# Rows of a routed expert turned later on TensorE, first weights of the second expert loaded ahead, and the last expert ended tile by tile

## The chip, the core and the metric

The kernel runs on one core of a Trainium2 chip. The core has a matrix engine (TensorE, in the rows PE, its weight loads PEld), VectorE (DVE), ScalarE (ACT), GpSimd (POOL) and SyncE (SP), which run side by side and wait for each other by semaphores. Each engine takes its instructions strictly in the order in which they stand in its program. SP issues most transfers, POOL the indirect ones (a list of row numbers says which rows are read or written). The metric is the device time of one launch in microseconds, lower is better; the median of three runs is given.

## The reference

A windowed attention, then a gated feed-forward layer, then a layer of eight experts of which each token uses two. The change lies at the joint of the second and the third and at the end of the third:

```python
g = xn @ w_gate                                # feed-forward, d_ff 1536
x = (g * sigmoid(g) * (xn @ w_val)) @ w_out    # 1536 tokens x 512
logits = x @ w_gate2 + log1p(exp(x @ w_noise)) * noise
top2, top2_w = two best of 8 experts, softmax over the two
for e in range(8):
    h = maximum(x[mask_e] @ w1[e], 0)          # 512 -> 1024
    out[mask_e] += top2_w * (h @ w2[e])        # 1024 -> 512
```

Every product is taken as three fp32r products (high and low halves of both operands).

## The kernel before

The feed-forward layer visits groups of 256 or 512 tokens with a chunk of its 12 weight blocks at a time; the last visit (`VISITS[-1]`, tokens 1280 to 1535, blocks 8 to 11) makes for each block f a product with `w_gate` and one with `w_val` (`up`, 12 matmuls each, L646), the gate on ACT and DVE (`hidden`), and one visit later the product with `w_out` (`down`, L672). After a group's last block `route` picks the experts of its tokens and scatters token number and weight into `metad`, one slot for each token and expert.

The experts are run as `Unit`s. Unit 0 holds the first 256 slots of the expert that led after three of the five groups, so that it can start while the last tokens are still being routed; unit 1 holds that expert's other 256 slots and needs the last group (`late_slots`). Units 2 to 8 are the other experts in order of their number of tokens (`order`), with 480 down to 368 slots. A unit's steps, whose names the rows use:

- `fetch` (L853): SP reads its slots from `metad` into `me`; `slots` (L862): POOL makes row numbers `ic`;
- `gather` (L871): POOL issues one indirect transfer of 128 rows of `x2d` into `xg`, for each tile of slots;
- `turn` (L881): four PE transposes of `xg` into a PSUM bank `pg`, then ACT makes the high half `gh` (L883) and DVE the low half `gl` (L884);
- `run`: for f in 0 to 7 an `up` (12 matmuls into `pz`, L907, that read `gh` and `gl` of all the unit's slots), ReLU into `zh`, `zl`, and one step later a `down` into `ac` (L929, or L923 in units of the wide form); then the weighting `y` (L961, L964) and the indirect write of `y` into the output (L965).

`moe2_weights` has SP load the 256 KB slabs of `w1` (L837) and `w2` (L840) for one f; `late` reads all seven expert numbers on SP (L1059). The calls `side(f)` put the next unit's fetch, gathers, turns and weights between the steps of the running one. That is only the order of priority: the tile scheduler builds the program of each engine by a simulated timeline of its own, so an instruction stands where that timeline had its inputs ready. `follow(a, b)` ties instruction a behind b on the same engine.

Three buffers matter: four `xg` tiles shared by consecutive units, two PSUM banks for `pg` (tags t and o), and 19 weight slabs.

## Time and profile before

| | us |
|---|---|
| median of three runs (818.26 to 821.02) | 820.84 |
| the profiled execution | 815.08 |
| its span | 812.9 |
| PE busy | 778.2 (96%) |
| DVE, ACT, POOL busy | 459.6, 362.6, 312.9 |

The span is from the first to the last instruction of the profiled execution; 2.2 us of its time lie around it. PE is busy 96% of the span, with matmuls whose ends are modelled, so what can be read exactly is where it stood idle and who released it. The granted clock is a mean over a stretch: 1.00 is 2.4 GHz and 0.50 is 1.2 GHz.

### The profile page before, as it was taken

How to read it: one execution, taken by the hardware profiler on the slowest of the kernel's cores; microseconds unless marked ns; L12 is line 12 of the kernel's file. 1: busy time of each engine (PE TensorE's matmuls, PEld its weight loads, DVE VectorE, ACT ScalarE, POOL GpSimd, SP SyncE). 2: the span in 40 equal slices, each digit the busy share in tenths (PEclk: the TensorE clock that was granted, in tenths of full speed). 3: DMA queues.
4: the chain of work that ended last, by engine and by line, in shares of the span. 5: the costliest groups of instructions: out<-in, count | busy, mean ns of one | idle time of the engine just before them, and what ended most of it. 6: DMA issues, size and time to landing. Idle time of an engine off the chain costs nothing. (4 is left out here: it accounts for less than half of the span.)

```text
span 812.9 us, 13827 instructions
## 1 busy us (share of the span) xinstructions
PE 778.2 (96%) x5041; PEld 696.2 (86%) x5041; DVE 459.6 (57%) x1053; ACT 362.6 (45%) x807; POOL 312.9 (38%) x353
## 2 busy tenths in 40 slices
PE   8999999999899999999997996999999999999993
PEld 5789999999788888899996985888999999999982
DVE  4489866667487887334453575533545454545541
ACT  5677656656443443123332463433333434344430
POOL 7437742232285565002421335342424343524311
PEclk9999999999999999999999999999999999999997
DMA  8465421260242330010108005973363728272010
GB/s 187 106 165 146 118 65 28 45 190 15 79 130 93 118 100 0 1 52 27 27 9 242 25 18 159 330 240 120 104 207 114 246 89 269 87 234 75 36 37 34
DMA packets 116838, 88.76 MB, mean 109 GB/s; under 512 B 49449, under 2 KB 100649, under 8 KB 116768
## 3 DMA queue, kind: packets, MB, share of 16 engines
q1 hardware_dynamic: 107920, 65.43, 28.7%
q0 software_dynamic: 7120, 19.27, 7.1%
q10 hardware_dynamic: 1728, 3.15, 1.3%
q8 instruction: 41, 0.67, 0.4%
q14 instruction: 29, 0.24, 0.1%
HBM read 75.18 MB, written 13.34 MB: 109 GB/s over the span
## 5 line engine op out<-in xcount | busy, mean ns | idle before, releaser
L907 PE MATMUL pz<-gh,sa 128*128 128x256 f32 (+7 forms) x576 | 157.6, 340 | 0.8 <-ACT gh L883 0.8
L907 PEld LDWEIGHTS pz<-gh,sa 128*128 128x128 f32 x576 | 104.2, 190 | 6.2 <-ACT gh L883 1.0
L907 PE MATMUL pz<-gl,sa 128*128 128x256 f32 (+7 forms) x288 | 97.8, 339 | 0.9 <-DVE gl L884 0.9
L672 PE MATMUL acc<-wo,dh 128*128 128x512 f32 x288 | 88.3, 400 | 0.8 <-ACT dh L658 0.8
L923 PE MATMUL ac<-zh,sb 128*128 128x480 f32 (+4 forms) x320 | 86.3, 364 | 0.0
L911 ACT ACTIVATE zh<-pz 128x256 fp32r<-128x256 f32 (+7 forms) x72 | 35.1, 487 | 110.0 <-PE pz L907 110.0
L912 DVE SCALAR_TENSOR_TENSOR zl<-pz,zh 128x256 fp32r<-128x256 f32 (+7 forms) x72 | 39.8, 553 | 75.1 <-ACT zh L911 74.8
L646 PE MATMUL pz<-xTh,wg 128*128 128x256 f32 x352 | 73.7, 288 | 1.2 <-ACT xTh L550 1.0
L646 PE MATMUL pz<-xTh,wv 128*128 128x256 f32 x352 | 73.9, 288 | 0.1
L628 ACT ACTIVATE sa<-wab 128x512 fp32r<-128x512 f32 x72 | 45.2, 629 | 57.9 <-PE ac L923 40.5
L632 DVE TENSOR_TENSOR sa<-wab,sa 128x512 fp32r<-128x512 f32 x51 | 36.6, 720 | 45.5 <-ACT sa L628 45.3
L646 PEld LDWEIGHTS pz<-xTh,wg 128*128 128x128 f32 x352 | 58.4, 192 | 3.5 <-ACT xTh L550 1.2
L923 PEld LDWEIGHTS ac<-zh,sb 128*128 128x128 f32 x320 | 57.9, 188 | 3.2
L672 PEld LDWEIGHTS acc<-wo,dh 128*128 128x128 f32 x288 | 51.3, 189 | 9.7 <-ACT dh L658 1.4
L646 PEld LDWEIGHTS pz<-xTh,wv 128*128 128x128 f32 x352 | 58.4, 192 | 0.8 <-ACT wv L599 0.5
L659 POOL TENSOR_TENSOR dl<-u,dh 128x256 fp32r<-128x256 f32 (+1 forms) x38 | 37.8, 996 | 53.0 <-ACT dh L658 44.7
L907 PEld LDWEIGHTS pz<-gl,sa 128*128 128x128 f32 x288 | 54.8, 190 | 3.8 <-DVE gl L884 1.1
L871 POOL DMA_INDIRECT xg<-x2d,ic x30 | 30.5, 1018 | 67.7 <-PE pg L881 61.3
L812 POOL DMA_INDIRECT metad<-meta,si x24 | 24.3, 1012 | 83.4 <-DVE si L791 77.3
L672 PE MATMUL acc<-wo,dl 128*128 128x512 f32 x144 | 53.0, 400 | 0.2 <-POOL dl L659 0.2
L923 PE MATMUL ac<-zl,sb 128*128 128x480 f32 (+4 forms) x160 | 52.9, 357 | 0.0
L632 DVE TENSOR_TENSOR sb<-wab,sb 128x512 fp32r<-128x512 f32 x67 | 47.1, 703 | 8.9 <-ACT sb L628 8.0
(268 smaller groups left out, 1872.4 us busy)
## 6 DMA issues: line engine op xcount, KB each, us to landing
wab<-in_moe_w_dram SPq DMA_DIRECT2D x128, 256.0 KB, 4.9
rg<-in_moe_w_gate_dram SPq DMA_DIRECT2D x12, 512.0 KB, 3.7
rv<-in_moe_w_val_dram SPq DMA_DIRECT2D x12, 512.0 KB, 3.7
ro<-in_moe_w_out_dram SPq DMA_DIRECT2D x12, 512.0 KB, 3.5
vn<-in_v_dram SPq DMA_DIRECT2D x12, 256.0 KB, 4.4
out_dram<-zero SPq DMA_DIRECT2D x1, 3072.0 KB, 12.8
x2d<-x ACTq DMA_DIRECT2D x12, 256.0 KB, 3.6
kn<-in_k_dram SPq DMA_DIRECT2D x11, 256.0 KB, 3.9
```

What stands on the lines that cost most here:

```text
L628: cp = nc.scalar.activation(wp[:, 0], src, AF.Copy)
L632: (nc.gpsimd if pool else nc.vector).tensor_sub(wp[:, 1], src, wp[:, 0].bitcast(F32))
L646: nc.tensor.matmul(pz, a[:, cs], x[:, tt:tt + nt, c, :], start=(n == 0), stop=(n == 3 * DC - 1))
L659: (nc.gpsimd if ci < len(CHUNKS) - 1 else nc.vector).tensor_sub(dl, u, dh.bitcast(F32))
L672: nc.tensor.matmul(acc[t], a[:, tt], w, start=(f == CHUNKS[ci][0] and n == 0), stop=(end and n == 2))
L812: st = nc.gpsimd.indirect_dma_start(out=metad, out_offset=bass.IndirectOffsetOnAxis(ap=si[:, t, kk:kk + 1], axis=0), in_=meta[:, G0[g] + t ...
L871: self.last = nc.gpsimd.indirect_dma_start(out=xg[:m], out_offset=None, in_=x2d[:self.rows], in_offset=bass.IndirectOffsetOnAxis(ap=self.i ...
L907: nc.tensor.matmul(pz[:, :cap], a[:, cs], x[:, c, :cap], start=(k == 0), stop=(k == 3 * DC - 1))
L911: nc.scalar.activation(dh[:, :cap], pz[:, :cap], AF.Relu)
L912: nc.vector.scalar_tensor_tensor(dl[:, :cap], pz[:, :cap], 0.0, dh[:, :cap].bitcast(F32), op0=ALU.max, op1=ALU.subtract)
L923: nc.tensor.matmul(acc[c][:, :cap], w[:, c * P:(c + 1) * P], a[:, :cap], start=(f == 0 and k == 0), stop=(f == FB2 - 1 and k == 2))
```

## The change

- `turn` takes a matmul `behind` and ties its transposes to it. Unit 0's two turns go from the places kx 3 and 4 (blocks 8 and 9 of the last visit) to blocks 10 and 11, each behind that block's last `w_val` product. Unit 2's four turns, which were asked for from f = 4 on, go behind the last `up` product of unit 1 at f = 6 (two) and f = 7 (two). Turns of the other units are asked for as before.
- `late` reads only one expert number and at once loads four f of unit 2's weights (eight slabs), before unit 2's slots are fetched. The other six numbers are read when their unit is first asked for.
- In the last unit (8, three tiles of slots) the third tile's columns are cut in two halves with a PSUM bank each, and the `down` products of f = 6 and 7 are held and issued tile by tile: tiles 0 and 1 for f = 6, then for f = 7, then the third tile's first half for both f, then its second half. The weighting of the third tile becomes two DVE instructions.

```diff
@@ -643,8 +643,9 @@
         for c in range(DC):
             cs = slice(c * P, (c + 1) * P)
             for a, x in ((wh, xTh[g]), (wh, xTl[g]), (wl, xTh[g])):
-                nc.tensor.matmul(pz, a[:, cs], x[:, tt:tt + nt, c, :], start=(n == 0), stop=(n == 3 * DC - 1))
+                mm = nc.tensor.matmul(pz, a[:, cs], x[:, tt:tt + nt, c, :], start=(n == 0), stop=(n == 3 * DC - 1))
                 n += 1
+        return mm.ins
 
     def hidden(ci, f, t0, nt, pg, pv):
         GN = nt * P
@@ -872,13 +873,15 @@
                 out=xg[:m], out_offset=None, in_=x2d[:self.rows], in_offset=bass.IndirectOffsetOnAxis(ap=self.ic[:m, s:s + 1], axis=0))
             self.xg[s] = xg
 
-        def turn(self, s):
+        def turn(self, s, behind=None):
             m = self.tiles[s][1]
             xg = self.xg.pop(s)
             pt = ps.tile([P, 512], F32, name=f"pg{self.n}_{s}", tag="to"[s % 2])
             p3 = pt.rearrange("p (a b) -> p a b", a=DC)[:, :, :m]
             for c in range(DC):
-                nc.tensor.transpose(p3[:, c, :], xg[:m, c * P:(c + 1) * P], ident[:m, :m])
+                mm = nc.tensor.transpose(p3[:, c, :], xg[:m, c * P:(c + 1) * P], ident[:m, :m])
+                if behind is not None:
+                    follow(mm.ins, behind)
             ss = slice(s * P, s * P + m)
             nc.scalar.activation(self.gh[:, :, ss], p3, AF.Copy)
             nc.vector.tensor_sub(self.gl[:, :, ss], p3, self.gh[:, :, ss].bitcast(F32))
@@ -892,9 +895,14 @@
 
         def run(self, side):
             n, cap, gh, gl = self.n, self.cap, self.gh, self.gl
+            ending = n == E and len(self.tiles) < 4
+
+            def cuts(s):
+
+                return (slice(0, DM // 2), slice(DM // 2, DM)) if ending and s + 1 == len(self.tiles) else (slice(0, DM),)
             wide = cap % P > 0 and cap > 2 * P and n < 8
             acc = [ps.tile([P, 512], F32, name=f"ac{n}_{s}", tag=("d", "d", "t2", "s")[s], bufs=(2, 2, 1, 1)[s])
-                   for s in range(DC if wide else len(self.tiles))]
+                   for s in range(DC if wide else len(self.tiles) + ending)]
             self.ys = {}
 
             def up(f):
@@ -904,8 +912,9 @@
                 for c in range(DC):
                     cs = slice(c * P, (c + 1) * P)
                     for a, x in ((wh, gh), (wh, gl), (wl, gh)):
-                        nc.tensor.matmul(pz[:, :cap], a[:, cs], x[:, c, :cap], start=(k == 0), stop=(k == 3 * DC - 1))
+                        mm = nc.tensor.matmul(pz[:, :cap], a[:, cs], x[:, c, :cap], start=(k == 0), stop=(k == 3 * DC - 1))
                         k += 1
+                self.mark = mm.ins
                 dh = pools["b"].tile([P, CAP], F32R, name=f"zh{n}_{f}", tag="dh", bufs=2)
                 dl = pools["b"].tile([P, CAP], F32R, name=f"zl{n}_{f}", tag="dl", bufs=2)
                 nc.scalar.activation(dh[:, :cap], pz[:, :cap], AF.Relu)
@@ -913,22 +922,42 @@
                                                op1=ALU.subtract)
                 return dh, dl
 
+            def products(f, d, ws, s, x, behind=None):
+                wh, wl = ws
+                m = self.tiles[s][1]
+                o = acc[s + x][:m, cuts(s)[x]]
+                for k, (a, w) in enumerate(((d[0], wh), (d[0], wl), (d[1], wh))):
+                    mm = nc.tensor.matmul(o, a[:, s * P:s * P + m], w[:, cuts(s)[x]], start=(f == 0 and k == 0),
+                                          stop=(f == FB2 - 1 and k == 2)).ins
+                    if behind is not None:
+                        follow(mm, behind)
+                        behind = mm
+                return mm
+
             def down(f, d):
-                wh, wl = split(f"b{self.wkey}_{f}", n)
+                ws = wh, wl = split(f"b{self.wkey}_{f}", n)
                 if n:
                     give(f"ab{self.wkey}_{f}")
+                if ending and f >= FB2 - 2:
+                    held.append((f, d, ws))
+                    if len(held) == 2:
+                        end = len(self.tiles) - 1
+                        turns = [(h, s, 0) for h in held for s in range(end)] + [(h, end, x) for x in range(2) for h in held]
+                        mm = None
+                        for h, s, x in turns:
+                            mm = products(*h, s, x, mm)
+                    return
                 if wide:
                     for c in range(DC):
                         for k, (w, a) in enumerate(((wh, d[0]), (wl, d[0]), (wh, d[1]))):
                             nc.tensor.matmul(acc[c][:, :cap], w[:, c * P:(c + 1) * P], a[:, :cap],
                                              start=(f == 0 and k == 0), stop=(f == FB2 - 1 and k == 2))
                     return
-                for s, m in self.tiles:
-                    ss = slice(s * P, s * P + m)
-                    for k, (a, w) in enumerate(((d[0], wh), (d[0], wl), (d[1], wh))):
-                        nc.tensor.matmul(acc[s][:m], a[:, ss], w, start=(f == 0 and k == 0),
-                                         stop=(f == FB2 - 1 and k == 2))
-
+                for s, _ in self.tiles:
+                    for x in range(len(cuts(s))):
+                        products(f, d, ws, s, x)
+
+            held = []
             prev = None
             for f in range(FB2):
                 d = up(f)
@@ -958,7 +987,9 @@
             for s, m in self.tiles:
                 if n > 1:
                     y = self.ys.pop(s)
-                    nc.vector.scalar_tensor_tensor(y[:m], acc[s][:m], mf[:m, s, 1:2], y[:m], op0=ALU.mult, op1=ALU.add)
+                    for x, cols in enumerate(cuts(s)):
+                        nc.vector.scalar_tensor_tensor(y[:m, cols], acc[s + x][:m, cols], mf[:m, s, 1:2], y[:m, cols],
+                                                       op0=ALU.mult, op1=ALU.add)
                 else:
                     y = sb.tile([P, DM], F32, name=f"y{n}_{s}", tag="acc", bufs=NACC)
                     nc.vector.tensor_scalar(y[:m], acc[s][:m], mf[:m, s, 1:2], None, op0=ALU.mult)
@@ -1035,7 +1066,7 @@
             count += 1
             up(f, "g", t0, nt, pg)
             side()
-            up(f, "v", t0, nt, pv)
+            vm = up(f, "v", t0, nt, pv)
             d = hidden(ci, f, t0, nt, pg, pv)
             side()
             if prev is not None:
@@ -1047,17 +1078,24 @@
                 units[0].slots()
                 units[0].gather(0)
                 units[0].gather(1)
-            if kx in (3, 4):
-                units[0].turn(kx - 3)
+            if (ci, t0) == VISITS[-1][:2] and f in CHUNKS[ci][-2:]:
+                units[0].turn(f - CHUNKS[ci][-2], vm)
             if kx is not None and kx < FB2 - 2:
                 moe2_weights(0, units[0].e, kx + 2)
     finish(*prev)
 
+    AHEAD = 4
+
+    def name(u):
+        u.e = nc.sync.value_load(order.bitcast(I32)[:1, u.n - 2:u.n - 1], min_val=0, max_val=E - 1)
+
     def late():
         route(NG - 1)
         for i in range(E - 1):
-            r = nc.sync.value_load(order.bitcast(I32)[:1, i:i + 1], min_val=0, max_val=E - 1)
-            units.append(Unit(2 + i, 1 + i, r, 0, CAPS[i]))
+            units.append(Unit(2 + i, 1 + i, None, 0, CAPS[i]))
+        name(units[2])
+        for f2 in range(AHEAD):
+            moe2_weights(1, units[2].e, f2)
     late()
 
     for i, u in enumerate(units):
@@ -1068,12 +1106,18 @@
             if nxt is not None:
                 if i:
                     if f == 0:
+                        if nxt.e is None:
+                            name(nxt)
                         nxt.slots()
                     if 1 <= f <= len(nxt.tiles):
                         nxt.gather(f - 1)
-                if 8 - len(nxt.tiles) <= f:
+                if i == 1:
+                    for s in range(len(nxt.tiles)):
+                        if f == 6 + s // 2:
+                            nxt.turn(s, u.mark)
+                elif 8 - len(nxt.tiles) <= f:
                     nxt.turn(f - 8 + len(nxt.tiles))
-            if nw is not None:
+            if nw is not None and (i > 1 or f >= AHEAD):
                 moe2_weights(nw.wkey, nw.e, f)
         u.run(side)
     fast.close()
```

TensorE, the last feed-forward visit, where the first turn of unit 0 (`pg0_0`) stands. Before:

```order
L646 MATMUL pz10_8_5439<-xTh2_2331,wg8_3760 128x256
L646 MATMUL pz10_8_5439<-xTh2_2331,wv8_3771 128x256
L646 MATMUL pz10_8_5439<-xTl2_2332,wv8_3771 128x256
L646 MATMUL pz10_8_5439<-xTh2_2331,wv8_3771 128x256 x2
L881 MATMUL pg0_0_5338<-ident_60,xg0_0_5202 128x128 x4
L646 MATMUL pz10_8_5439<-xTl2_2332,wv8_3771 128x256
L646 MATMUL pz10_8_5439<-xTh2_2331,wv8_3771 128x256 x2
L646 MATMUL pz10_8_5439<-xTl2_2332,wv8_3771 128x256
```

After, at the new place of the same turn:

```order
L673 MATMUL acc3_10_5581<-wo9_3915,dh10_9_5577 128x512 x2
L673 MATMUL acc3_10_5581<-wo9_3915,dl10_9_5578 128x512
L673 MATMUL acc3_11_5582<-wo9_3915,dh10_9_5577 128x512 x2
L673 MATMUL acc3_11_5582<-wo9_3915,dl10_9_5578 128x512
L882 MATMUL pg0_0_5628<-ident_60,xg0_0_5202 128x128 x4
L646 MATMUL pz10_11_5635<-xTh2_2331,wg11_4109 128x256
L646 MATMUL pz10_11_5635<-xTl2_2332,wg11_4109 128x256
L646 MATMUL pz10_11_5635<-xTh2_2331,wg11_4109 128x256 x2
```

The turn moved from the middle of block 8's `w_val` products behind the `down` of block 9, past the products of blocks 9 and 10 and three `down`s; `pg0_1` stands one block later.

TensorE, unit 1, where the turns of unit 2 (`pg2_0` to `pg2_3`) stand. Before, the first of them:

```order
L907 MATMUL pz1_3_6239<-gl1_5783,sa0_3_1_6236 128x256
L907 MATMUL pz1_3_6239<-gh1_5782,sa0_3_1_6236 128x256
L881 MATMUL pg2_0_6292<-ident_60,xg2_0_6188 128x128 x4
L929 MATMUL ac1_0_6137<-sb0_2_1_6261,zh1_2_6218 128x512
L929 MATMUL ac1_1_6138<-sb0_2_1_6261,zh1_2_6218 128x512
L929 MATMUL ac1_0_6137<-sb0_2_1_6261,zh1_2_6218 128x512
```

After, the first two of them:

```order
L915 MATMUL pz1_6_6285<-gh1_5782,sa0_6_1_6282 128x256
L882 MATMUL pg2_0_6302<-ident_60,xg2_0_6143 128x128 x4
L882 MATMUL pg2_1_6309<-ident_60,xg2_1_6174 128x128 x4
L930 MATMUL ac1_0_6095<-sb0_5_1_6319,zh1_5_6266 128x512
L930 MATMUL ac1_1_6096<-sb0_5_1_6319,zh1_5_6266 128x512
```

Further on, the last two, the first products of unit 2 (`pz2`) and the first turn of unit 3 (`pg3_0`):

```order
L930 MATMUL ac1_1_6096<-sb0_6_1_6365,zl1_6_6299 128x512
L882 MATMUL pg2_2_6348<-ident_60,xg2_2_6205 128x128 x4
L882 MATMUL pg2_3_6355<-ident_60,xg2_3_6236 128x96 x4
L930 MATMUL ac1_0_6095<-sb0_7_1_6374,zh1_7_6344 128x512 x2
L930 MATMUL ac1_1_6096<-sb0_7_1_6374,zh1_7_6344 128x512 x2
L930 MATMUL ac1_0_6095<-sb0_7_1_6374,zl1_7_6345 128x512
L930 MATMUL ac1_1_6096<-sb0_7_1_6374,zl1_7_6345 128x512
L915 MATMUL pz2_0_6400<-gh2_6121,sa1_0_2_6397 128x480
L915 MATMUL pz2_1_6438<-gh2_6121,sa1_1_2_6435 128x480
L882 MATMUL pg3_0_6577<-ident_60,xg3_0_6455 128x128 x4
L915 MATMUL pz2_0_6400<-gl2_6122,sa1_0_2_6397 128x480
L915 MATMUL pz2_0_6400<-gh2_6121,sa1_0_2_6397 128x480 x2
```

Unit 2's first turn moved from behind `up` 3 to behind `up` 6 of unit 1. Unit 3's first turn, which stood behind the whole of `up` 0 and `up` 1 of unit 2, now stands behind their first two products, though the code asks for it as before.

SyncE, behind the fetch of unit 1's slots. Before, the numbers of all seven experts are read here:

```order
L853 DMA me1_5560<-metad_111 128x2x2
L1059 TENSOR_LOAD order_138
...
L853 DMA me2_6159<-metad_111 128x4x2
L837 ISA
L837 DMA wab1_0_6165<-in_moe2_w1_dram 128x4x128
```

After:

```order
L854 DMA me1_5546<-metad_111 128x2x2
L1090 TENSOR_LOAD order_138
L1090 ISA x2
L838 ISA
L838 DMA wab1_0_5825<-in_moe2_w1_dram 128x4x128
...
L841 DMA wab1_3_5834<-in_moe2_w2_dram 128x512
L854 ISA
L854 DMA me2_6117<-metad_111 128x4x2
```

Seven reads ahead of unit 2's fetch became one read and eight weight transfers.

## Rows read from the trace of the kernel before

**Rows 1.** Page, busy time by engine
```profile
PE 778.2 (96%) x5041; PEld 696.2 (86%) x5041; DVE 459.6 (57%) x1053; ACT 362.6 (45%) x807; POOL 312.9 (38%) x353
```

**Rows 2.** Waits of PE: for whom, us in total, times, longest
```profile
PE pg L881 <- DMA xg<-x2d,ic: 11.5, 3, 5.1
```

**Rows 3.** Timeline of PE, 440 to 465 us: start, length, operation, idle before
```profile
440.40 1.09 PE L881 MATMUL pg<-ident,xg 128*128 128x128 f32 x4 [5.14 <-DMA xg<-x2d,ic]
...
464.50 0.62 PE L672 MATMUL acc<-wo,dl 128*128 128x512 f32 x2
```

**Rows 4.** Timeline of PE, 474 to 520 us
```profile
489.23 0.63 PE L881 MATMUL pg<-ident,xg 128*128 128x128 f32 x4 [1.28 <-DMA xg<-x2d,ic]
...
492.45 0.50 PE L907 MATMUL pz<-gh,sa 128*128 128x256 f32 x2 [0.77 <-ACT gh L883]
493.85 0.39 PE L907 MATMUL pz<-gl,sa 128*128 128x256 f32 x1 [0.90 <-DVE gl L884]
...
499.47 0.28 PE L907 MATMUL pz<-gh,sa 128*128 128x256 f32 x1
...
500.89 0.85 PE L929 MATMUL ac<-sb,zh 128*128 128x512 f32 x3
...
502.28 0.28 PE L907 MATMUL pz<-gh,sa 128*128 128x256 f32 x1
...
508.89 1.09 PE L881 MATMUL pg<-ident,xg 128*128 128x128 f32 x4 [5.03 <-DMA xg<-x2d,ic]
```

**Rows 5.** Windows behind the three waits: busy by engine, granted clock, DMA share, GB/s
```profile
440.40:443.80 3.40, 3.40 (x14) 3.25 (x15) 0.85 (x2) 0.98 (x2) 0.00 (x0) 0.50 1.03 328
495.00:498.40 3.40, 3.40 (x17) 3.30 (x16) 1.12 (x2) 1.27 (x4) 0.72 (x1) 0.50 0.41 154
508.70:512.10 3.40, 3.21 (x10) 2.76 (x11) 0.69 (x1) 0.60 (x1) 0.00 (x0) 0.50 1.07 354
```

**Rows 6.** Timeline of POOL, 501 to 504 us
```profile
501.96 1.07 POOL L871 DMA_INDIRECT xg<-x2d,ic  x1 [0.47 <-POOL ic L862]
503.33 1.34 POOL L871 DMA_INDIRECT xg<-x2d,ic  x1 [0.30 <-issue]
```

**Rows 7.** Timeline of SP, 498 to 514 us
```profile
498.50 0.37 SPq L853 DMA_DIRECT2D me<-metad  x1
499.13 0.37 SPq L837 DMA_DIRECT2D wab<-in_moe_w_dram  x1
...
513.52 0.37 SPq L853 DMA_DIRECT2D me<-metad  x1
```

**Rows 8.** Transfers issued at 492.2, 422.9, 498.5, and from 499 to 515 us: median to landing
```profile
metad<-meta,si POOLq DMA_INDIRECT x1, 6.3
metad<-meta,si POOLq DMA_INDIRECT x1, 7.7
me<-metad SPq DMA_DIRECT2D x1, 4.0 KB, 2.7
xg<-x2d,ic POOLq DMA_INDIRECT x4, 7.6
me<-metad SPq DMA_DIRECT2D x1, 4.0 KB, 5.4
```

**Rows 9.** Waits of SP's queue, 484 to 600 us
```profile
SPq L853 <- DMA metad<-meta,si: 5.9, 1, 5.9
```

**Rows 10.** Timeline of DVE, 488 us: the order of the experts is written
```profile
488.23 0.16 DVE L830 FIND_INDEX8 order<-c,cnt 128x8 uint32<-128x8 f32 x1
```

**Rows 11.** Timeline of PE, DVE and POOL at the end
```profile
797.98 0.84 PE L929 MATMUL ac<-sb,zl 128*128 128x512 f32 x3
798.40 2.07 DVE L961 SCALAR_TENSOR_TENSOR y<-ac,me,y 128x512 f32<-128x512 f32 x3 [2.64 <-PE ac L929]
799.43 1.01 POOL L965 DMA_INDIRECT out_dram<-y,me  x1 [22.01 <-DVE y L961]
...
802.05 0.96 POOL L965 DMA_INDIRECT out_dram<-y,me  x1 [0.30 <-issue]
```

## The prediction

> **What bounds the kernel now.** The page comes first: PE is busy 96% of the span [rows 1], so the question is where the missing time stands. Then PE's waits: one entry dwarfs the rest, three waits of the turns (`pg`) for gathered rows, 11.5 us together [rows 2]. The timeline places them: 5.14 us ahead of unit 0's first turn, 1.28 us ahead of unit 1's, 5.03 us ahead of unit 2's [rows 3, 4]. PE works in order, so products that stand behind a turn and need nothing of it wait too. Third, the clock: after each of these places stands a stretch of 3.4 us at a granted 0.50, that is 1.2 GHz, while PE is full [rows 5]; each costs about 1.7 us (the third 1.6, 0.2 us of it being the wait itself). Last, the path of the rows: POOL's gather needs `ic`, `ic` needs `me`, and unit 2's `me` was fetched at 498.50, just when the last scatter of slots landed: issued at 492.2, plus 6.3, is 498.5, and SP stood 5.9 us for it. The first gather follows 3.46 us after the fetch [rows 6 to 9].
>
> I work on the profiled execution (815.08 us, span 812.9). It is 5.8 us below the median of the timed runs, 820.84; nothing in one trace tells where those 5.8 us lie, so I take the same saving off the median.
>
> **First turn (unit 0).** In the old order PE stops at 440.40 - 5.14 = 435.3 and the rows come at 440.4 [rows 3]. In the new order it has block 9, block 10 and three `down`s first. A 256-column product starts every 0.118 us and a 512-column one every 0.23 us (twelve and six of them fill 499.47 to 500.89 and 500.89 to 502.28) [rows 4]. So 7 products are left of block 8, two blocks have 48, three `down`s 18: 55 x 0.118 + 18 x 0.23 = 10.6 us, plus the last-but-one group's routing. The turn is reached after 445.9, and the rows land at 440.4: no wait. Gone are 5.14 us and the slow stretch, 1.7 us. What is late next: unit 0's first `up` needs ACT's and DVE's halves of the second turn. At unit 1 this handover cost 0.77 and 0.90 us, with the turn directly ahead of the `up` [rows 4]; here four products of 0.23 us stand between, and two more ahead of the first one that reads `gl`. I take 0.3 us (0 to 1.7). Term: 5.14 + 1.7 - 0.3 = 6.5 us (5.1 to 6.8).
>
> **Turn of unit 1.** The chain from the last tokens' `down` (its end at 464.96, [rows 3]) through routing, slots and gather to the turn at 489.23 takes 24.3 us, and PE had 23.0 us of work beside it, hence 1.28 us of wait [rows 4]. In the new order the last `down` stands behind only two products of unit 0's first two `up`s, where all 24 stood ahead of it: 22 x 0.118 = 2.6 us more cover. The wait should go; I take 1.0 us (0 to 1.28), since this chain shares DVE and ACT with unit 0. The 0.77 and 0.90 us behind it stay, as that turn is placed as before. Whether the slow stretch at 495.0 stays with them the trace can't say: between 0 and 1.7 us, I take 0.8.
>
> **Turns of unit 2.** I use the old clock of unit 1, since the whole stage slides with PE. Reading one number in place of seven does not bring the fetch of `me` forward, as it had the scatter to wait for in any case [rows 9]. The eight weight transfers now run beside that scatter. With no weights in flight it took 6.3 us, in the earlier case with weights 7.7 us [rows 8]. So `me` is issued between 498.5 and 499.9, and the first gather between 502.0 and 503.4; it lands 7.6 us later, at 509.6 to 511.0, the second at 510.9 to 512.3 [rows 6, 8]. PE, not stopped at 503.86, has three `up`s and three `down`s more, 3 x 2.81 = 8.4 us [rows 4], and comes to the first turn at 512.3, or 510.6 if the slow stretch of the last paragraph goes; the second follows 0.36 us later. The wait is 0 to 1.4 us; I take 0.6. The other two turns stand 4.9 us further on. Term: 5.03 + 1.6 - 0.6 = 6.0 us (5.2 to 6.6; below that by rival 1).
>
> **First turn of unit 3.** It now stands behind two products of unit 2, where 24 stood ahead of it. PE reaches it 7.4 us after the end of `up` 6: two turns 0.7, `down` 5, `up` 7, `down` 6 4.2, two turns 0.65, `down` 7 1.4, two products 0.44. That is 519.7 (518.0). Its fetch follows unit 2's after eight weight issues, nine steps of 0.63 us [rows 7], and one number of 0.6 us (seven fit between 488.4 and the start of the 5.9 us wait at 492.6, [rows 9, 10]): 504.8 to 506.2. It lands 5.4 us later, as the one at 513.52 did; the gather is 3.46 - 2.7 = 0.76 us behind it [rows 6 to 8] and takes 7.6 us: 518.6 to 520.0. If the eight back up as the sixteen ahead of 513.52 did (14.4 us, so 7.2), the rows land at 520.7 to 522.1. The wait is 0 to 4 us; I take 1.0, near the unhindered issue because half as many transfers stand in the queue.
>
> **The end.** The last weighting is three DVE instructions in 2.07 us from 798.40, then POOL issues three writes 1.31 us apart, the last at 802.05 [rows 11]. In the new order tile 0 is complete nine products of 0.23 us after `down` 6 begins, tile 1 three later, against 15 and so on before: about 1.6 us earlier. PE's own end stays, as 256 columns cost half of 512. POOL then starts near 797.7, and its third write at 800.3, when the second half has been weighted (PE's end 798.8, some 0.7 us). 802.05 - 800.3 = 1.8 us (0 if the drain behind POOL doesn't move, 2.1 at most). The extra PSUM bank and the 24 extra PE instructions cost nothing I can see. The five reads of numbers now sit on SP inside unit 2's stage, 3 us of its queue, ahead of weights that unit 3 needs 40 us later.
>
> **Sum.** 6.5 + 1.0 + 0.8 + 6.0 - 1.0 + 1.8 = 15.1 us: 820.84 - 15.1 = 805.7 (on the profiled execution 800.0). Best bounds 6.8 + 1.3 + 1.7 + 6.6 - 0 + 2.1 = 18.5, giving 802.3; worst 5.1 + 0 + 0 + 5.2 - 4 + 0 = 6.3, giving 814.5.
>
> The slow stretches are 3.4 us of the 15.1, read from the granted 0.50 behind the first and the third wait [rows 5]. The Trainium skill, "TensorE: Matmul & The Clock Gate", section "What's actually happening", advises to leave the ramp out of a model since it is under 1% of a typical span. By that advice the sum would be 11.7 us without the sure stretches and 10.9 without the doubtful one too. The trace agrees on the size (5 us of 812.9 is 0.6%) but not on the use: here it is a fifth of what is forecast, so I keep it.
>
> **Rivals.** 1. The waits move to the new places. For: turns go where a simulated timeline thinks the rows have landed, and that timeline put unit 2's turn 5.03 us too early; unit 3's now stands even nearer to its gather. Against: 8.4 us more of PE work ahead of unit 2's. Price: 2.5 us more at unit 2, 3 us more at unit 3, and a slow stretch of 1.7 us: 805.7 + 7.2 = 812.9. What could make it so is traffic beside the scatter and the gathers: the scatter took 1.4 us longer with weights in flight [rows 8]. The Trainium skill, "DMA: Bandwidth & Descriptors", section "Queues, rings and completion order", states that each transfer engine takes turns between its queues packet by packet, so weights loaded early would slow both; by that rule, too, a scatter is slowed and not stopped behind 2 MB of weights, and these rows agree.
> 2. The handover binds: ACT's and DVE's halves of the last turn hold up the first `up` of units 0 and 2, 1.67 us and a slow stretch of 1.7 us at each as at unit 1, less the 0.3 counted: 805.7 + 6.4 = 812.1. Against: four and six products stand between.
> 3. The routing chain, not PE, sets unit 1's start. If it gains 4 us less than PE, the wait becomes 2.7 us in place of 0.3: with the slow stretch, 805.7 + 2.4 + 0.8 = 808.9.
> 4. Slower: the third expert's rows. If the fetch of unit 3's slots, which also waits for the output rows of unit 0 whose buffer it takes, stays where it was on the clock (513.52, rows landed at 513.52 + 5.4 + 0.76 + 7.6 = 527.3), PE, which by the first two places is 8.3 us ahead and so comes there at 519.7 - 8.3 = 511.4, waits 15.9 us instead of 1.0, with 1.7 us of slow clock: 805.7 + 16.6 = 822.3. From a landing at 530 on the kernel is slower by over 0.5%. Against: the fetch has eight transfers ahead of it, not sixteen.
>
> **How the numbers follow.** Forecast 0.70, rival 1 0.13, rival 2 0.05, rival 3 0.06, rival 4 0.06, of it half with no change and half slower. 0.5% (4.1 us) is about what a measurement of this kernel can tell from no change. The forecast and rivals 1 to 3 all stay below 816.7: faster 0.93 with a remainder of 0.01 for mixtures to no change, same 0.04, slower 0.03. The range reaches from the best sum, 802, to rival 1, 812.9.
>
> **What would show it.** Right: PE's waits for `xg` fall from 11.5 us to under 2.5; the stretches at 0.50 behind the first and third place are gone; unit 2's fetch still ends a wait for the scatter; POOL's last write is issued some 1.8 us earlier against PE's last product. Wrong: a wait for `xg` or for `gh` and `gl` of over 2 us at unit 2 or 3, a scatter that lands more than 8 us after its issue, or the end of POOL's drain at the same distance from PE's last product.

## The result and the profile after

The changed kernel takes 809.38 us (median of 4 runs, 807.32 to 810.02) against 819.74 us for the kernel before on the same chip: ratio 0.987, 95% interval 0.9841 to 0.9898, a gain of 10.4 us. Run again later beside fresh runs of before it gave 806.94 against 817.04, ratio 0.9888 (0.987 to 0.9906), 10.1 us. Forecast were 805.7 us and a gain of 15.1. The direction and the range held; a third of the gain did not come.

Of the profile after, first the page's busy time and the waits of PE (columns as in [rows 1, 2]).

```profile
PE 776.0 (96%) x5065; PEld 694.6 (86%) x5065; DVE 459.0 (57%) x1054; ACT 363.2 (45%) x807; POOL 313.1 (39%) x353
```
```profile
PE pg L882 <- DMA xg<-x2d,ic: 7.3, 4, 3.2
```

PE's share is what it was. Its waits for gathered rows fell from 11.5 us to 7.3, not to the "under 2.5" that the prediction names as the sign of success. PE's timeline shows which are gone (start, length, operation, idle before).

```profile
449.52 0.60 PE L882 MATMUL pg<-ident,xg 128*128 128x128 f32 x4
...
455.50 1.20 PE L673 MATMUL acc<-wo,dh 128*128 128x512 f32 x4 [0.46 <-ACT dh L659]
...
456.78 0.63 PE L673 MATMUL acc<-wo,dl 128*128 128x512 f32 x2
...
474.07 0.50 PE L915 MATMUL pz<-gh,sa 128*128 128x256 f32 x2 [1.01 <-DVE sa L632]
...
484.01 0.63 PE L882 MATMUL pg<-ident,xg 128*128 128x128 f32 x4 [0.86 <-DMA xg<-x2d,ic]
...
492.35 1.20 PE L930 MATMUL ac<-sb,zh 128*128 128x512 f32 x4 [0.91 <-ACT zh L920]
...
509.43 0.63 PE L882 MATMUL pg<-ident,xg 128*128 128x128 f32 x4 [2.77 <-DMA xg<-x2d,ic]
510.57 0.63 PE L882 MATMUL pg<-ident,xg 128*128 128x128 f32 x4 [0.51 <-DMA xg<-x2d,ic]
...
521.21 0.63 PE L882 MATMUL pg<-ident,xg 128*128 128x128 f32 x4 [3.20 <-DMA xg<-x2d,ic]
```

Unit 0's turn, which waited 5.14 us [rows 3], waits for nothing at 449.52; two small waits behind it are new (0.46 us for `dh`, the high half of the last block's gate, and 1.01 us for a weight half `sa`). Unit 1's first turn waits 0.86 where it waited 1.28 [rows 4], and one of its `down`s waits 0.91 us for `zh`. Unit 2's turns wait 2.77 + 0.51 = 3.28 us where the first waited 5.03 [rows 4]. And there is a new wait, 3.20 us at unit 3's first turn, two products into unit 2.

Behind the last of them, at unit 3, stands the only stretch at a granted 0.50 that this part of the execution still has (window, PE, PEld, DVE, ACT and POOL busy, granted clock, DMA share, GB/s); of the three of [rows 5] none is left at its old place.

```profile
486.20:489.70 3.50, 1.88 (x14) 1.44 (x13) 2.33 (x4) 0.98 (x2) 2.65 (x3) 1.00 0.93 198
522.10:525.50 3.40, 3.40 (x10) 2.82 (x9) 0.69 (x1) 0.37 (x1) 2.03 (x2) 0.50 1.09 345
```

Why unit 2's rows are late is read on POOL and SP (timelines of the two).

```profile
487.20 0.98 POOL L813 DMA_INDIRECT metad<-meta,si  x1 [0.30 <-issue]
...
501.67 0.23 POOL L863 TENSOR_SCALAR ic<-me 128x4 int32<-128x4 int32 x1 [10.93 <-DMA me<-metad]
502.38 1.28 POOL L872 DMA_INDIRECT xg<-x2d,ic  x1 [0.47 <-POOL ic L863]
```
```profile
483.73 0.37 SPq L838 DMA_DIRECT2D wab<-in_moe_w_dram  x1
...
488.94 0.01 SPq L841 DMA_DIRECT2D wab<-in_moe_w_dram  x1
499.70 0.37 SPq L854 DMA_DIRECT2D me<-metad  x1
...
506.75 0.00 SPq L854 DMA_DIRECT2D me<-metad  x1
```

The last scatter of slots is issued at 487.20 and the fetch of `me` that waits for it goes out at 499.70: 12.5 us, where it was 492.2 to 498.5, 6.3 us, before [rows 7, 8]. Eight weight transfers (four pairs of 2 x 256 KB) are issued from 483.73 to 488.94 and move beside it.

The end: PE's last product starts at 795.43 and ends at 795.71; POOL's last write is issued at 797.30, 1.59 us later, where it was 3.23 us [rows 11].

```profile
793.65 1.87 DVE L991 SCALAR_TENSOR_TENSOR y<-ac,me,y 128x512 f32<-128x512 f32 x3 [0.99 <-PE ac L930]
795.74 0.48 DVE L991 SCALAR_TENSOR_TENSOR y<-ac,me,y 112x256 f32<-112x256 f32 x1 [0.22 <-PE ac L930]
...
797.30 0.96 POOL L996 DMA_INDIRECT out_dram<-y,me  x1 [0.30 <-issue]
```

### The profile page after: what moved, and what is told of

Read it like the earlier page. It is cut to its first block, busy times and chain, and to the rows that moved or that the text cites. A ratio compares the mean times of both kernels' runs of the same rounds, so it can differ in the third digit from the quotient of the medians.

```text
span 808.2 us, 13871 instructions
## 1 busy us (share of the span) xinstructions
PE 776.0 (96%) x5065; PEld 694.6 (86%) x5065; DVE 459.0 (57%) x1054; ACT 363.2 (45%) x807; POOL 313.1 (39%) x353
## 4 chain that ended last, share of the span: by engine, by line
PE 78%; issue 8%; DMA 5%; POOL 4%; ACT 2%; DVE 2%; POOLq 0%; SPq 0%; ACTq 0%
PE pz L915 15%; PE pz L646 13%; PE ac L953 12%; PE acc L673 11%; PE pv L646 5%; PE pg L646 5%; PE ps L403 3%; PE ac L930 3%; PE pp L425 2%; DMA rv<-in_moe_w_val_dram 2%; PE po L476 1%; PE po L472 1%; PE lg L732 1%; PE pg L882 1%; PE pt L362 1%
## 5 line engine op out<-in xcount | busy, mean ns | idle before, releaser
L673 PEld LDWEIGHTS acc<-wo,dh 128*128 128x128 f32 x288 | 51.2, 188 | 10.4 <-ACT dh L659 2.1
L813 POOL DMA_INDIRECT metad<-meta,si x24 | 24.3, 1013 | 87.1 <-DVE si L792 81.0
```

Source lines behind the costliest of these rows:

```text
L673: nc.tensor.matmul(acc[t], a[:, tt], w, start=(f == CHUNKS[ci][0] and n == 0), stop=(end and n == 2))
L813: st = nc.gpsimd.indirect_dma_start(out=metad, out_offset=bass.IndirectOffsetOnAxis(ap=si[:, t, kk:kk + 1], axis=0), in_=meta[:, G0[g] + t ...
```

## The experiments

Three sets of runs, each beside the kernel before on its own chip; ratios are to that. Sets 1 and 3 ran on one chip, set 2 on another, where before is faster (814.1 us against 818.6 and 817.0).

**1. The kernel before, a second profile.** No edit.

> The kernel before, unchanged, for the spread of its own waits between two profiled executions. The gain by the two medians is 10.4 us (819.7 to 809.4), by the two profiled executions only 5.1 us (815.1 to 810.0). If the missing 5 us are the spread of the profiled execution of before, this one has TensorE's three waits for gathered rows again (11.5 us together, 3.2 to 5.1 us each) and two stretches at granted 0.50 more than the changed kernel, and its time lies nearer 820 than 815. If something in before's program is slower on some executions, one of its waits is longer by several us here.

Measured 818.79 us. Its waits for rows are longer than the first profile's.

```profile
PE pg L881 <- DMA xg<-x2d,ic: 13.1, 3, 6.1
...
PE lg L758 <- issue: 1.3, 1, 1.3
```

These are 1.6 us more, and the second row, a wait in the routing that the first profile doesn't have, 1.3 us; of the 3.7 us between the two profiles that is most. (The waits of the first were 5.14, 1.28 and 5.03 us; the "3.2" of the expectation is none of them.) The clock differs as well: behind the first wait, which ends at 442.3, the granted 0.50 lasts until 447.9, 5.5 us and not 3.4, and behind unit 1's turn there is none. So the first profile was a short one, and the gain between the two profiled executions (5.1 us) understates the change.

**2. The changed kernel without weights ahead.**

```
-    AHEAD = 4
+    AHEAD = 0
```

> The changed kernel, with no weight pair of unit 2 fetched ahead of its slots (all eight are fetched by unit 1's side work, as in the kernel before). Theory 1, the four pairs slow the scatter of the slots: SP's wait on the slots' scatter falls from 10.0 to about 6 us, the scatter lands 6 to 8 us after its issue and not 12.4, unit 2's rows are there some 4 to 5 us sooner, TensorE's wait of 3.28 us at unit 2's turns goes, and the time is 805 to 808 (0.995 to 0.998 of the changed kernel) if unit 3's wait of 3.20 us moves with it, else about 806 to 809. Rival A, the scatter is slow whatever runs beside it (its own spread from 6 to 12 us): the waits stay at 2.8 and 3.2 us and the time is 809 to 810. Rival B, without the weights ahead unit 2's first up products wait for weights: a wait for wab stands at unit 2's start and the time is 811 or more.

Measured 807.21 us, 0.9875 (0.9843 to 0.9907). That lies in theory 1's range, but the changed kernel takes the same on that chip (806.94, 0.9888). Yet nearly everything that theory 1 said of the rows came true, as POOL, SP and PE show in turn.

```profile
488.08 0.98 POOL L813 DMA_INDIRECT metad<-meta,si  x1 [0.31 <-issue]
...
515.05 0.24 POOL L863 TENSOR_SCALAR ic<-me 128x4 int32<-128x4 int32 x1 [11.49 <-DMA me<-metad]
515.82 1.54 POOL L872 DMA_INDIRECT xg<-x2d,ic  x1 [0.53 <-POOL ic L863]
517.66 0.95 POOL L872 DMA_INDIRECT xg<-x2d,ic  x1 [0.30 <-issue]
518.62 1.27 POOL L632 TENSOR_TENSOR sa<-wab,sa 128x512 fp32r<-128x512 f32 x1
```
```profile
494.48 0.37 SPq L854 DMA_DIRECT2D me<-metad  x1
```
```profile
507.37 0.63 PE L882 MATMUL pg<-ident,xg 128*128 128x128 f32 x4 [0.56 <-DMA xg<-x2d,ic]
...
519.95 1.17 PE L915 MATMUL pz<-gh,sa 128*128 128x480 f32 x2 [4.88 <-POOL sa L632]
```

The scatter is back at 6.4 us (488.08 to 494.48) and unit 2's turns wait 0.56 us in place of 3.28. But 4.88 us stand a few products later, at unit 2's first weight block, with a granted 0.54 from 520.0 to 523.4 behind them. It looked like rival B, weights too late. POOL says otherwise: the subtraction that makes the low half of that block (`sa`, line 632) is ready to run but stands in POOL's order behind unit 3's `ic`, which sat 11.49 us idle for `me`, and two gathers. I had not seen this queue before the run; it became theory 2.

**3. Unit 2's weights held behind its gathers.** All eight pairs are fetched after the last gather of rows has been issued.

```
+        if behind is not None:
+            follow(nc.gpsimd.memset(raw[f"ab{u}_{f}"][:1, :, :1], 0.0).ins, behind)
...
+            if i == 1:
+                if f == len(nxt.tiles):
+                    for f2 in range(FB2):
+                        moe2_weights(nw.wkey, nw.e, f2, nxt.last.ins)
```

> The changed kernel, but all eight weight pairs of unit 2 are held until its four gathers of rows have been issued on GpSimd (a write of one column by GpSimd into each slab, ordered behind the last gather). No weight runs beside the scatter or beside the gathers. Theory 1: scatter at 6 us from issue, and the gathers land faster than with weights beside them, so TensorE doesn't wait at unit 2's turns; 805 to 808 if the weights, fetched some 12 us later, are still in time. Rival A: waits for rows as in the changed kernel, 809 to 810. Rival B, the weights are late at unit 2's start: TensorE waits for the first slab there, by up to 5 us, 810 to 814.

Measured 813.60 us, 0.9946 (0.9927 to 0.9964): slower than the changed kernel. The time is rival B's, the cause isn't: PE waits 10.92 us, again for POOL's half and not for the weights.

```profile
511.06 0.63 ACT L628 ACTIVATE sa<-wab 128x512 fp32r<-128x512 f32 x1 [0.54 <-issue]
```
```profile
520.42 0.23 POOL L865 TENSOR_SCALAR ic<-me 128x4 int32<-128x4 int32 x1 [17.35 <-DMA me<-metad]
...
523.49 1.27 POOL L632 TENSOR_TENSOR sa<-wab,sa 128x512 fp32r<-128x512 f32 x1
```

ACT made the high halves of unit 2's first two blocks at 509.90 and 511.06, so the weights had landed; POOL's low half of the first block starts at 523.49, because unit 3's `me` is now fetched later still and POOL stands 17.35 us for it.

**4. The same, with unit 3's turns tied.**

```
-                    nxt.turn(f - 8 + len(nxt.tiles))
+                    nxt.turn(f - 8 + len(nxt.tiles), u.mark if i == 2 else None)
```

> As the kernel that holds unit 2's weights behind the gathers, and unit 3's turns as well are tied each behind an up product of unit 2 (at steps 4 to 7, where the changed kernel ties only unit 2's). Theory 1: if unit 3's wait of 3.20 us comes of its fetch and gathers standing late behind unit 2's, a turn tied to the same steps waits as before and the time equals that of the kernel without this edit. Rival C, the wait at unit 3 comes from where its turns stand in TensorE's order (pulled up ahead of up products that are ready): the wait goes, and with it the 3.4 us stretch at granted 0.50 behind it, and the time is 4 to 5 us under that of the kernel that holds the weights alone, 801 to 804.

Measured 812.25 us, 0.9941 (0.992 to 0.9961): the same as experiment 3, with 9.90 us at the same place. Neither theory 1 nor rival C is decided by it; the wait for POOL's half covers both.

**5. The changed kernel with unit 3's turns tied** (the line of experiment 4 alone).

> The changed kernel, and unit 3's four turns are tied each behind an up product of unit 2 (steps 4 to 7); in the changed kernel the first of them stands two products into unit 2, where TensorE waited 3.20 us for its rows, with 3.4 us at granted 0.50 behind it. Theory 1a (that wait is the turn's place and nothing stands under it, since GpSimd's half of unit 2's first weight block was ready at 518.05 and TensorE would have needed it at about 518.0): the wait and the slow stretch go, 809.4 less 4.9 = 804.5 (803.5 to 805.5). Rival D (GpSimd's half of the weights is next in line): a wait for sa of 2 us or more takes the place of the wait for rows, with a slow stretch, 808 to 809.5.

Measured 803.44 us, 0.9862 (0.984 to 0.9884), at the lower edge of theory 1a's 803.5 to 805.5, though on the chip where before is faster too; by the ratio it is only 0.1 to 0.3% ahead of the changed kernel, inside the intervals. The trace is clearer: no wait at unit 3's turn and none for POOL's half (rival D fails), waits for rows 2.6 us in all. The profiled execution (805.12 us; the six runs reach from 800.3 to 805.2) still has two stretches at a granted 0.50, 490.0 to 493.4 behind unit 1's turn and 510.5 to 513.7 behind unit 2's.

```profile
PE pg L882 <- DMA xg<-x2d,ic: 2.6, 3, 1.4
```

So the 3.20 us were the turn's place; what its removal is worth in time these runs don't show. The scatter, with weights beside it, took 10.0 us here (487.44 to 497.48).

**6. No weights ahead, and unit 2's halves on VectorE.**

```
-        pool = u == 0 and f < 5 if key[0] == "b" else u >= 2 and f < 3
+        pool = u == 0 and f < 5 if key[0] == "b" else u > 2 and f < 3
```

> The changed kernel without weights ahead, and the second halves of unit 2's first three weight blocks are made by VectorE in place of GpSimd. Without this edit (807.2) TensorE waited 4.88 us at unit 2's first block for GpSimd, whose queue had unit 3's list (5.7 us for its slots to arrive) and two gathers ahead of the half. Theory 2 (GpSimd's queue is what holds unit 2 there, not the weights' arrival): the wait falls under 1.5 us and the 3.4 us at granted 0.50 behind it goes, 807.2 less 5 = 802.2 (801 to 804). Rival B (the weights land late): the same wait stands at VectorE's half and the time stays at 806 to 808. Rival E (VectorE is full there): waits of 2 us or more for VectorE's own work, 805 to 808.

Measured 803.58 us, 0.9877 (0.9859 to 0.9894). The wait for POOL's half is gone and no other for weights took its place: theory 2 holds, rivals B and E fall. But the time didn't come down as theory 2 said (its ratio is that of experiment 2, 0.9875), since a third wait stood behind: PE reaches unit 3's first turn sooner and waits 3.77 us there.

```profile
518.95 1.09 PE L882 MATMUL pg<-ident,xg 128*128 128x128 f32 x4 [3.77 <-DMA xg<-x2d,ic]
```

**7. The same, with unit 3's turns tied** (experiments 2, 6 and 4 together).

> As the kernel with unit 2's halves on VectorE and no weights ahead, and unit 3's turns tied behind unit 2's up products as well. By theory 2, TensorE comes to unit 3's first turn about 5 us sooner than before that edit, so an early place of the turn would wait for its rows (gathered from 515.8 on, landed at about 523): if the other kernel shows that wait, this one is 2 to 5 us faster than it, 799 to 802; if it doesn't, both agree within 1 us.

Measured 800.35 us, 0.9827 (0.981 to 0.9844); 3.2 us less than experiment 6 in the same set, within its 2 to 5. The one wait for rows left is unit 1's.

```profile
PE pg L882 <- DMA xg<-x2d,ic: 0.9, 1, 0.9
```

This kernel beats both: its interval lies below that of the changed kernel (0.987 to 0.9906 in set 3; the first measurement's, 0.9841 to 0.9898, it just touches), though the two ran on different chips.

**8. Unit 0's turns alone.** The kernel before, with these turns placed and tied as in the change.

```
-            if kx in (3, 4):
-                units[0].turn(kx - 3)
+            if (ci, t0) == VISITS[-1][:2] and f in CHUNKS[ci][-2:]:
+                units[0].turn(f - CHUNKS[ci][-2], vm)
```

> The kernel before with unit 0's two turns alone tied behind the last two blocks' products; units 1 to 3, the weights and the end are as before. By the forecast's terms 6.5 us for the wait at 440 and 1.0 plus 0.8 for unit 1's turn, if nothing later takes it back: 818.6 less 6.5 to 8.3 = 810.3 to 812.1. Rival F (the gain is taken back by unit 2's turn, whose rows hang on the same lists: the wait of 5 to 6 us there grows by what PE gained): the wait at unit 2 is 9 us or more and the time is 815 or more.

Measured 808.60 us, 0.993 (0.9916 to 0.9944), a gain of 5.5 us (4.6 to 6.8), a little under the 6.5 to 8.3 expected. The wait is gone; unit 2's is 5.66 us, as before and not 9, so rival F falls. Two sizes fell short: the waits of 0.45 and 1.02 us behind unit 0's turns are new here too, and behind unit 2's wait the granted 0.50 lasted from 502.3 until 509.4, so some 3 us were lost to it in this execution in place of 1.6 [rows 5].

**9. The changed kernel again.**

> The changed kernel itself, for its ratio on the same chip as the three single edits, and for a second trace of its waits. Theory 1 (four pairs in flight slow the slots' scatter): the scatter lands 10 to 12.5 us after its issue again, where seven runs without weights ahead have 5.3 to 6.8 us, and TensorE waits 2 to 4 us at unit 2's turns and 2 to 4 us at unit 3's. Rival A (the 12.5 us were one execution's): it lands after 6 to 8 us and the waits are under 1 us.

Measured 806.94 us, 0.9888 (0.987 to 0.9906). The scatter takes 11.9 us (issued 485.04, `me` fetched at 496.90), so rival A falls. Unit 2's turns wait 1.77 + 0.79 = 2.56 us; unit 3's turn only 1.15 us, and that for DVE.

```profile
518.21 0.63 PE L882 MATMUL pg<-ident,xg 128*128 128x128 f32 x4 [1.15 <-DVE y L995]
```

**10. The weights ahead alone, in the kernel before.** SP's part of the change: one expert number read, four pairs of unit 2 fetched there.

```
+        name(units[2])
+        for f2 in range(AHEAD):
+            moe2_weights(1, units[2].e, f2)
```

> The kernel before with the weights ahead alone (four pairs of unit 2 fetched ahead of its slots, one expert number read for seven): the turns and the end are as before. Theory 1: the scatter lands 4 to 6 us later than before's 6.3, the rows of unit 2 with it, and TensorE's wait there grows from 5.0 to some 9 us (before's trace: 5.03; 6.12 in its second): 1.003 to 1.006 of the kernel before. Theory of the change as forecast (nothing but SP's order moves, the scatter slows by 1.4 us at most): 0.999 to 1.002, the wait at 5 to 6.5 us. Rival G (weights there sooner free unit 2's start by more than the rows cost): 0.995 to 0.998.

Measured 813.07 us, 0.9966 (0.9945 to 0.9987): theory 1's loss didn't come, rival G's side is right, but not for its reason. The scatter took 7.8 us (492.46 to 500.30), though the same eight transfers were issued around it (489.51 to 493.56); why it was slowed less than in the changed kernel stays open. The edit isn't one part alone: the scheduler puts a turn where its simulated transfers have landed, and with more transfers ahead it moved unit 2's first turn by itself from behind unit 1's `up` 3 to behind `up` 6. There it doesn't wait.

```profile
512.47 0.60 PE L881 MATMUL pg<-ident,xg 128*128 128x128 f32 x4
```

The same effect works on unit 3: its first turn stands two products into unit 2 with the weights ahead and 24 products in without (experiment 2: at 526.11), in this kernel as in the changed one.

**11. Unit 2's turns alone**, tied as in the change; the rest as before.

```
-                if 8 - len(nxt.tiles) <= f:
+                if i == 1:
+                    for s in range(len(nxt.tiles)):
+                        if f == 6 + s // 2:
+                            nxt.turn(s, u.mark)
+                elif 8 - len(nxt.tiles) <= f:
                     nxt.turn(f - 8 + len(nxt.tiles))
```

> The kernel before with unit 2's four turns alone tied behind unit 1's up products 6 and 7, no weights ahead. The forecast's term: the wait of 5.0 to 6.1 us and its slow stretch go, 6.0 us or 0.9925 of the kernel before. Theory 2 (GpSimd's queue is next in line: unit 3's list and two gathers ahead of the half of unit 2's first weight block): a wait for sa of 3 to 5 us with a slow stretch takes its place 3 us behind the turns, and only 0 to 2.5 us are gained, 0.997 to 1.000.

Measured 815.88 us, 0.9984 (0.9966 to 1.0002): not the forecast's 0.9925, but theory 2's. Of 5 us of wait 2.00 stay at unit 2's second turn, and 2.51 us for POOL's half are new, a little under theory 2's 3 to 5.

```profile
PE pz L910 <- POOL sa L632: 2.5, 1, 2.5
```

**12. The changed kernel without the new end.**

```
-            ending = n == E and len(self.tiles) < 4
+            ending = False
```

> The changed kernel with the last expert's end as before (no tile-by-tile order of the last two blocks, no halves). The two traces have GpSimd's last write 3.23 us behind TensorE's last product before and 1.59 us after, so this one should be 1.6 us slower than the changed kernel beside it (1.002; forecast 1.8). Rival H (the drain of the rows written sets the end, not their issue): no difference, within 0.5 us.

Measured 806.27 us, 0.9885 (0.9862 to 0.9907): no difference in time. In the trace POOL's last write is issued 3.23 us behind PE's last product, as before, against 1.60 us in the changed kernel beside it (PE's end 791.17, write at 792.77).

```profile
788.37 0.84 PE L930 MATMUL ac<-sb,zl 128*128 128x512 f32 x3
```
```profile
792.44 0.97 POOL L996 DMA_INDIRECT out_dram<-y,me  x1 [0.30 <-issue]
```

What hides the 1.6 us lies ahead of the end, where the edit changes nothing: PE is done 1.96 us sooner in this execution than in experiment 9 (789.21 against 791.17). Unit 3's first turn stands two products into unit 2 in both, but doesn't wait here, where it waited 1.15 us.

```profile
516.28 0.60 PE L882 MATMUL pg<-ident,xg 128*128 128x128 f32 x4
```

And there is one stretch at 0.50 (508.2 to 511.5) where experiment 9 has two (487.2 to 490.7 and 508.0 to 511.2), against 1.25 us more of waits at unit 2's turns (2.59 + 1.22). In both profiles the span ends 10.9 us behind the issue of the last write (803.3 and 803.7), so by the traces the new end is worth 1.6 us after PE; the times, which differ by less than their intervals, can't show it apart, and rival H, which expected no difference, isn't refuted by them.

## Why the prediction was right in sign and too large

By the signs that the prediction named, two of "wrong" came: waits for `xg` of over 2 us at units 2 and 3, and a scatter that landed more than 8 us after its issue. The table sets the terms beside the two profiles of the changed kernel (us gained against [rows 2 to 5, 11], worked out from the waits above and the stretches at 0.50, each at half its length).

| term | forecast | first profile | second profile |
| --- | --- | --- | --- |
| unit 0's turn | 6.5 | 5.4 | 5.4 |
| unit 1's turn, wait | 1.0 | 0.4 | 0.4 |
| unit 1's turn, clock | 0.8 | 1.7 | 0 |
| unit 2's turns | 6.0 | 3.3 | 2.3 |
| unit 3's first turn | -1.0 | -4.9 | -1.1 |
| end | 1.8 | 1.6 | 1.6 |
| sum | 15.1 | 7.5 | 8.6 |

**First turn (unit 0): right, 1.1 us too large.** The wait and the stretch behind it are gone (6.84 us). The handover, taken at 0.3 us, cost nothing: unit 0's first `up` waits neither for `gh` nor for `gl`. What was lost are two waits that the sum didn't have, 0.46 us for `dh` and 1.01 us for `sa`; both stand in experiment 8 too and not in the kernel before. Alone the turn gave 5.5 us.

**Turn of unit 1: half right.** The wait fell by 0.4 us, not 1.0. PE had 25.9 us beside the chain in place of 23.0 (1.0 of them the wait for `sa`), so the cover grew about as reckoned. But the chain grew too: from the end of the last `down` (457.25, behind the two at 456.78) to the turn at 484.01 it takes 26.8 us, where the forecast held it at 24.3; why isn't shown. So the chain still sets unit 1's start, but the 2.7 us of rival 3 did not come. Whether the slow stretch stays was left open in the forecast, and is: the first profile has none, the second has one from 487.2 to 490.7, behind the same waits. In the first, PE then waits 0.91 us for `zh` at unit 1's first `down`, so 0.8 of the 1.7 us are left there.

**Turns of unit 2: the step that failed.** It priced the scatter of the slots at 6.3 to 7.7 us with weights beside it [rows 8]. With the four pairs in flight it took 12.5 us in the first profile and 11.9, 10.0 and 10.7 in experiments 9, 5 and 12, all in the changed order, but 7.8 in experiment 10; in nine profiles without them 5.3 to 7.0. The wait of 0.6 us that the step took is what experiment 2 measured (0.56) with the scatter at 6.4. The 7.7 us came from a scatter earlier in the kernel, with two weight transfers issued beside it (422.81 and 423.42) and not eight, and I took it as the end of the range.

**First turn of unit 3: mis-sized, and incomplete.** The turn was put in the right place, but a wait of 3.20 us and 1.7 us of slow clock stood there in place of 1.0 in the first profile; its fetch went out at 506.75 and PE was at the turn at 518.0. The fetch followed unit 2's by 7.05 us (6.2 in the second profile) where 6.3 were reckoned, so most of its lateness is the slow scatter handed on. Experiment 5 shows that the wait is the place. What the forecast didn't see at all is POOL: the low half of unit 2's first weight blocks stands behind unit 3's `ic` and gathers. With the weights ahead that costs nothing: the first of them is done at 518.05, just as PE comes, and in experiment 5, where PE isn't held at unit 3's turn, no wait for it shows. Without them, and with unit 2's turns tied, the half comes late (experiments 2, 3, 4, 11), and where that wait is taken away unit 3's turn waits (experiment 6). So two faults of the weights ahead (a slow scatter, an early turn) stand against one merit (unit 3's slots are fetched sooner, 506.75 against 509.35 in experiment 2, hence POOL is free sooner): with and without them the kernel takes the same time within the intervals (0.9888 and 0.9875). That these three alone make up the balance is argued from the waits, not shown.

**The end: right by the traces** (1.6 us for 1.8), not shown by the times.

So rival 1's mechanism, given 13%, is what happened at units 2 and 3. In the first profile its prices held too: 2.7 us more at unit 2 and 2.2 more at unit 3 (2.5 and 3 supposed) and a slow stretch. Its gain, 15.1 - 7.2 = 7.9 us, lies near both sums of the table; the medians, 10.1 to 10.4, lie between it and the forecast. Rival 2 did not come: at units 0 and 2 no `up` waits for `gh` or `gl`. Rival 4 did not come: the fetch went out at 506.75, not 513.52. The sums stand against 5.1 and 9.6 us between the profiled executions. The first has the 1.3 us of routing wait of experiment 1, which before's first profile lacks, and the 0.9 us for `zh`; with them its sum is 5.3 and closes. The 1.0 us that the second has over its sum stays open. That the medians say 10.1 to 10.4 fits before's spread (815.1 and 818.8 us in its two profiles), but no run shows where those us lie.

On the rules weighed before: the Trainium skill, "DMA: Bandwidth & Descriptors", section "Queues, rings and completion order", has the engines take turns between queues, so that a scatter is slowed and not stopped by loads beside it. The runs agree: with 2 MB in flight it took 7.8 to 12.5 us in place of 5.3 to 7.0. "TensorE: Matmul & The Clock Gate" of the Trainium skill, section "What's actually happening", says that for modeling the ramp penalty is under 1% of a typical kernel span. That did not fit the use here: the stretches behind these waits lasted from 3.2 to 6.1 us, up to 3 us of loss each, beside a gain of 10 us.

## What to carry to other kernels

When a transfer is moved ahead of a short, latency-bound one (a scatter whose landing starts a chain), price the short one with that traffic beside it, not from a quiet row. When a wait of an in-order engine is removed, read the queues of every engine that feeds the next few instructions for what stands ahead there: here a vector operation on GpSimd sat behind another unit's index fetch, and when that wait was taken away the next one showed. Under a scheduler that places work by its own simulated times, an edit of transfers also moves instructions, so an experiment on one part has to be read with its new order.

## What the runs showed of the hardware

- The clock doesn't follow from the waits alone. At unit 1's first turn and behind it stand waits of 0.86, 0.77 and 0.85 us (0.86 in the second) in both profiles of the changed kernel; the first kept full clock (486.20 to 489.70 above), the second fell to half for 3.5 us. Of the fourteen profiles six have such a stretch there and eight have none:

```profile
487.20:490.70 3.50, 3.50 (x19) 3.50 (x18) 1.12 (x2) 0.95 (x3) 1.08 (x2) 0.55 0.60 118
```

- The half-clock stretch behind a wait of 5 to 6 us is not one length: 3.4 us in the first profile of before [rows 5], 5.5 us behind the first wait of its second profile, and in experiment 8 most of these 6.3 us:

```profile
503.30:509.60 6.30, 6.30 (x24) 5.66 (x25) 1.38 (x2) 1.42 (x3) 0.00 (x0) 0.54 1.09 311
```

- A scatter by GpSimd of a few bytes per row is slowed by bulk loads: in the changed order 10.0 to 12.5 us from its issue to the fetch that waits for it beside 2 MB of weights, 6.4 us when only those loads are left out (experiment 2). The amount alone doesn't set it: with the same loads it took 7.8 us in experiment 10.
